# Attention row maxima moved on-chip by one transfer from ScalarE, projections planned half a unit sooner, and another order of the first loads

## The chip, the cores and the metric

The kernel runs on one core of a Trainium2 chip. The time is the device time of one execution in microseconds (us). The core has five engines, each with a queue of its own that it works through in order: TensorE (PE, with its weight loads shown apart as PEld), VectorE (DVE), ScalarE (ACT), GpSimd (POOL) and SyncE (SP). In this kernel SP computes nothing; it issues the DMA transfers. An instruction waits on semaphores for what it needs, and whatever stands behind it in its queue waits with it.

## The reference

Two layers, each of an attention with a compressed memory and a feed-forward part, on x of 2048 rows by 512 columns in float32:

```python
x = x + _A_ref(_layernorm(x, axis=-1), A_wq, A_wk, A_wv, A_wo, A_beta)
x = x + _B_ref(_layernorm(x, axis=-1), B_w_gate, B_w_up, B_w_down)   # (silu(x@wg) * (x@wu)) @ wd, F = 1792
# the same two lines again, with the same weights
```

`_A_ref` projects to q, k and v with 32 heads of 16, and cuts the 2048 rows into 4 segments of 512. Within a segment it is causal softmax attention; across segments each head keeps a 16 by 16 memory that it reads before and updates after a segment. The two results are mixed by a gate, and projected by wo.

## The kernel before, in words

**Precision.** Matmul operands are split into a high and a low part of a reduced format, so each projection takes three passes (`mm3`, L281): 12 matmuls of 128 by 512 for one q or k projection of one group of heads.

**Units.** A layer's attention is 32 units (s, n, h): 4 segments, 4 groups of 8 heads, 2 halves of 4 heads. Here they are counted from 0. Both halves of a group use the same q and k projection. The steps of a unit u are these:

- `qk_proj` (L454) is called for the group two ahead: q in an even unit, k in an odd one. PE makes the 12 matmuls, ACT copies the result out of PSUM (L464), POOL splits it (L465, L467), and SP writes it to a DRAM buffer scrq or scrk, first one part (L479), then two (L480).
- `load3` (L486) reads it back on SP, arranged by heads, into one of three on-chip buffers: cq in two transfers (L504; the trace calls that tile s) and ck in two (L509). As there are three, the load for unit u must wait until the last matmul of unit u-3 has read them.
- `mx_units` (L514) makes the score matmuls for the row maxima (L527); DVE reduces them (L534). `fin` (L541) has PE transpose the 16 by 128 maxima (L544), ACT negate them (L546), and SP write them to DRAM (L547, tile scrm) and read them back as one row of 2048 values into row 127 of cq (L548). That row takes the maximum off the scores in the next matmul.
- `at_units` (L555) makes the transposed score matmuls (L576) into three PSUM banks `plt`, ACT takes their exp (L582), POOL masks the diagonal blocks (L590), and PE multiplies by v (L609).

The feed-forward part (`up`, L856; `down`, L884) is long rows of 512-column matmuls (L866, L893); its first steps and its weight loads (L822) are mixed into the last units of the attention.

**What sets the order.** Nothing is issued as it is written. Every operation is recorded with a cost and a priority, which is a place in time: `at(v)` sets it to v times a unit length T. The tables OFF and PRE (L30, L31) hold these places in units, TA and TF (L29) the lengths for the two parts. `Program.issue` (L144) then plays the program through: on each engine, of the operations that are ready by its own clock, the one with the lowest priority is issued next. The latencies in LAT (L38) and the transfer time in `dma` (L274) say when a result counts as ready. So a changed cost or place reorders all five queues. The start of the first layer loads wv, x, wq, wk and wo (L717 to L728).

Of the kernel before, what the change touches and what calls it, by code (L numbers as in the profile page):

```python
# [8 lines left out]
F32 = mybir.dt.float32  # L9
# [16 lines left out]
LPW = 3  # L26
WOT = ("pmx_0", "pmx_1", "pj", "pj")
EARLY_AT = (23, 25, 26)
TA, TF = 13.82, 15.6  # L29
OFF = {'qe': (0.481, 1.468), 'at': (0.378, 1.18), 'mx': (-0.666, 0.16), 'lf': (-0.709, -0.318), 'mr': (0.865, 0.781), 'mu': (0.556, 0.139), 'wo': (0.263, 1.746), 'qk': (0.158, 0.91), 'v': (-0.3, 0.518), 'lp': (0.034, 1.108)}  # L30
PRE = {'c': -1.851, 'mb': 0.212, 'lv': -2.738, 'lo': -0.87, 'gate': -1.0, 'v': -1.534, 'dv': 0.12, 'qk1': -1.2, 'mx': -1.0}  # L31
EP = {'w': -1.935, 'wn': 0.178, 'ln': -3.0, 'dn': -0.06, 'up': -2.73}
POOL_W = ""
TABLE = 1.28
# [4 lines left out]
    pe=dict(pe=0.01, act=0.2, dve=0.2, sp=0.19),  # L39
    act=dict(act=0.22, dve=0.13, pe=0.27, pool=0.2, sp=0.15),  # L40
    dve=dict(dve=0.13, act=0.13, pe=0.25, pool=0.16, sp=0.12),
    pool=dict(pool=0.1, dve=0.06, pe=0.13, act=0.1, sp=0.05),
    sp=dict(act=0.91, dve=0.91, pe=0.95, pool=0.91, sp=0.91),
)


# [15 lines left out]


class Op:
    __slots__ = ("table", "mode", "eng", "cost", "lat", "fn", "prio", "bufs", "succ", "deps", "ready", "need", "wait", "index")

    def __init__(self, eng, cost, lat, fn, prio, bufs):
        self.eng, self.cost, self.lat, self.fn, self.prio, self.bufs = eng, cost, lat, fn, prio, bufs
        self.mode, self.table = None, None
        self.succ, self.deps, self.ready, self.need, self.wait = [], set(), 0.0, None, 0  # L70


class Program:
# [70 lines left out]
    def issue(self):  # L144
        for b in {id(b): b for o in self.ops for b in o.bufs if b.tag in self.shared}.values():
            first = b.ops[0].index
            need = {d for o in b.ops for d in o.deps if d.index < first}
# [8 lines left out]
        t = dict.fromkeys(engs, 0.65)  # L156
# [8 lines left out]
        done, bus, table, mode = 0, 0.0, "exp", "full"  # L165
        while done < len(self.ops):
            best = None
            for e in engs:
                f, n = fut[e], now[e]
                while True:  # L170
                    while f and f[0][0] <= t[e] + 1e-9:
                        _, i, o = heapq.heappop(f)
                        heapq.heappush(n, (o.prio, i, o))
                    if n:
                        o = n[0][2]
                        b = o.need
                        if b is not None and b.slot is None:
                            if not free[b.tag]:
                                heapq.heappop(n)
                                held[b.tag].append(o)  # L180
                                continue
                            fr = min(free[b.tag])
                            if fr[0] > t[e] + 1e-9:
                                heapq.heappop(n)
                                o.ready = fr[0]
                                heapq.heappush(f, (o.ready, o.index, o))
                                continue
                        start = t[e]
                    elif f:
                        start = f[0][0]  # L190
                        if best is None or start < best[0]:
                            t[e] = start
                            continue
                    else:
                        start = None
                    break
                if start is not None and n and (best is None or start < best[0]):
                    best = (start, e)
            assert best is not None, "no instruction can issue"
            start, e = best  # L200
            n = now[e]
            o = n[0][2]
            heapq.heappop(n)
            b = o.need
            if b is not None and b.slot is None:
                fr = min(free[b.tag])
                free[b.tag].remove(fr)
                b.slot = fr[1]
            for b in o.bufs:
                if b.tile is None:  # L210
                    tag = b.tag if b.slot is None else f"{b.tag}_{b.slot}"
                    b.tile = b.pool.tile(list(b.shape), b.dtype, name=tag, tag=tag)
            o.fn()
            done += 1
            t[e] = start + o.cost
            if o.table and o.table != table:
                table = o.table
                t[e] += TABLE
            if o.mode and o.mode != mode:
                t[e] += DRAIN[mode, o.mode]  # L220
                mode = o.mode
            end = t[e]
            if o.lat:
                bus = max(bus, end + 0.65) + o.lat
                end = bus
            for b in o.bufs:
                b.left -= 1
                if b.left == 0 and b.slot is not None:
                    free[b.tag].append((end + 0.25, b.slot))
                    for w in held[b.tag]:  # L230
                        w.ready = max(w.ready, end + 0.25)
                        heapq.heappush(fut[w.eng], (w.ready, w.index, w))
                    held[b.tag] = []
            for s in o.succ:
                s.ready = max(s.ready, end + LAT[e].get(s.eng, 0.0))
                s.wait -= 1
                if s.wait == 0:
                    heapq.heappush(fut[s.eng], (s.ready, s.index, s))
# [3 lines left out]
def infini_swiglu(ctx: ExitStack, tc: tile.TileContext, x, wq, wk, wv, wo, beta, wg, wu, wd, out,  # L242
                  layers=LAYERS, nseg=NSEG, do_ffn=True):
    nc = tc.nc
    xrows = x.rearrange("b s d -> (b s) d")
    orows = out.rearrange("b s d -> (b s) d")
    pool = ctx.enter_context(tc.tile_pool(name="sb", bufs=1))
# [3 lines left out]
    P = Program({"pj": 2})  # L251
# [20 lines left out]
        op("pool", cost, fn, reads, writes)  # L272

    def dma(fn, reads, writes, kb=256, cost=0.475):  # L274
        op("sp", cost, fn, reads, writes, lat=max(kb / 360, 0.02))

    def mm(ps, view, a, av, b, bv, n, start, stop, passes=1, rk=(None, None)):
        pe(n, passes, lambda: nc.tensor.matmul(view(ps.ap), lhsT=av(a.ap), rhs=bv(b.ap), start=start, stop=stop),  # L278
# [113 lines left out]
    def attention(lay, x_in, x_out, slots, T, hook):  # L392
# [121 lines left out]
        def mx_units(u):  # L514
            f_ = HLF[u]
            cq, ck = f_["cq"], f_["ck"]
            mx = sb("mx", [128, 4, 4], ring=2)

            def head(p, j):
                def f():  # L520
                    for grp in ((0, 1), (2,), (3,)):
                        ps = bank("pmx", ring=2)

                        def fill(ps=ps, grp=grp):
                            for a, qt in enumerate(grp):
                                nk = max(256, 128 * (qt + 1))
                                nc.tensor.matmul(ps.ap[:, a * 256:a * 256 + nk],  # L527
                                                 lhsT=cq.ap[0:127, 2 * j + p, qt * 128:(qt + 1) * 128],
                                                 rhs=ck.ap[0:127, p, 0:nk], start=True, stop=True)
                        pe(384 if grp == (2,) else 512, 1, fill, [(cq, j), (ck, 0), (ck, 1)], [ps], loads=len(grp))  # L530
                        for a, qt in enumerate(grp):
                            w = 128 * (qt + 1)
                            junk = sb("junk", [128, 512], BF16, ring=2)
                            dve(w, lambda a=a, qt=qt, w=w, ps=ps, junk=junk: nc.vector.tensor_tensor_reduce(  # L534
                                out=junk.ap[:, :w], in0=ps.ap[:, a * 256:a * 256 + w], in1=amask.ap[:, 512 - w:],
                                scale=1.0, scalar=-3e38, op0=OP.add, op1=OP.max,
                                accum_out=mx.ap[:, 2 * j + p, qt:qt + 1]),
                                [(ps, a), amask], [junk, (mx, (qt, p, j))])
                return f

            def fin():  # L541
                ps, nm = bank("pj"), sb("nm", [16, 128], F32R, ring=2)
                scr = P.buf(dram, "scrm", [16, 128], F32, ring=2)
                pe(128, 2, lambda: nc.tensor.transpose(ps.ap[:16, 0:128], mx.ap.rearrange("p t h -> p (t h)"),  # L544
                                                       ident.ap), [mx, ident], [ps])
                act(128, lambda: nc.scalar.mul(nm.ap, ps.ap[:16, 0:128], -1.0), [ps], [nm])  # L546
                dma(lambda: nc.sync.dma_start(scr.ap, nm.ap.bitcast(F32)), [nm], [scr], kb=8)  # L547
                dma(lambda: nc.sync.dma_start(  # L548
                    cq.ap[127:128].bitcast(F32).rearrange("o x c -> o (x c)"),
                    scr.ap.rearrange("(o x) c -> o (x c)", o=1)), [scr], [(cq, "m")], kb=8)  # L550
            return [head(p, j) for p in range(2) for j in range(2)] + [fin]

        PARTS = (((0, 0, 0, 512, 0),), ((1, 128, 0, 384, 1), (3, 384, 384, 128, 1), (2, 256, 0, 256, 2)))
# [450 lines left out]
```

## Time and profile before

| what | value |
|---|---|
| median of the three timed runs | 2023.94 us (2022.66 to 2025.35) |
| the profiled execution's own time | 2028.21 us |
| its span, first to last instruction | 2026.3 us |
| mean granted clock of TensorE | 0.994 |
| busy: PE, DVE, ACT, POOL | 1946.7, 1154.0, 770.7, 466.3 us |
| share of the DMA queue's packets in 16 engines' span | 29.7% |

In the lines of a profile, a group shows its line in the kernel, the engine, the operation, and the tiles as out<-in. A row of waits gives who waited for whom, and then the total, the number and the longest, in us. SPq is SP's queue. A row of the timeline begins with start and length in us; a bracket at its end says how long the engine had been idle and what ended that. A row of the table by stretches gives the stretch, its length, then for PE, PEld, DVE, ACT and POOL the busy time and the number of instructions, and at the end the granted clock, the DMA engines' share and GB/s.

### The profile page before, as it was taken

Reading aid. Unit: us, or ns where it says so; the run is one execution under the profiler, and the core shown is the slowest. Engines: PE = TensorE matmul, PEld = TensorE weight load, DVE = VectorE, ACT = ScalarE, POOL = GpSimd, SP = SyncE. Lnnn points to the kernel's source line nnn. Section 1 sums busy time; section 2 is a strip of 40 time slices with the busy share of each in tenths; the row PEclk is TensorE's granted clock in tenths of the full one; section 3 lists DMA queues with packets and bytes.
Section 4 is the critical chain, followed back from the end, with each engine's and each line's share of the span. In section 5 each row is a group of like instructions: output and inputs, shape, how many; then the busy total and the mean of one; then the engine's idle time right before and its main releaser. Section 6 shows DMA issues by size and latency. Waiting matters only on the chain. (4 is left out here: it accounts for less than half of the span.)

```text
span 2026.3 us, 31532 instructions
## 1 busy us (share of the span) xinstructions
PE 1946.7 (96%) x11136; PEld 1481.4 (73%) x11136; DVE 1154.0 (57%) x3446; ACT 770.7 (38%) x1758; POOL 466.3 (23%) x731
## 2 busy tenths in 40 slices
PE   6999999999999999999999899999989999999999
PEld 5667676766678888888866667666757788888887
DVE  5867777767744333333557667776686533333333
ACT  4555565545622212121235545554555212211211
POOL 5333433434410000000233334343343100000000
PEclk9999999999999999999999999999999999999999
DMA  7333434456231100010353344444462301100002
GB/s 221 120 111 119 140 106 142 122 156 190 63 115 32 32 21 18 25 32 21 104 194 111 95 129 124 132 136 122 142 184 64 111 14 32 32 21 11 16 1 83
DMA packets 101677, 184.54 MB, mean 91 GB/s; under 512 B 12880, under 2 KB 28240, under 8 KB 101456
## 3 DMA queue, kind: packets, MB, share of 16 engines
q1 hardware_dynamic: 101520, 182.52, 29.7%
q8 instruction: 89, 1.46, 0.3%
q14 instruction: 68, 0.56, 0.1%
HBM read 114.84 MB, written 67.63 MB: 90 GB/s over the span
## 5 line engine op out<-in xcount | busy, mean ns | idle before, releaser
L534 DVE CUSTOM_DVE_ANT_0 junk<-pmx,amask 128x128 bf16<-128x128 f32 (+3 forms) x1024 | 460.8, 484 | 162.2 <-PE pmx L527 154.2
L866 PE MATMUL plt<-s,s 128*128 128x512 f32 x1872 | 542.9, 395 | 0.0
L278 PE MATMUL pj<-s,s 128*128 128x512 f32 x1416 | 502.4, 410 | 1.4 <-DVE s L898 1.1
L582 ACT ACTIVATE s<-plt 128x512 f32<-128x512 f32 (+2 forms) x768 | 326.3, 464 | 231.3 <-PE plt L576 222.0
L866 PEld LDWEIGHTS plt<-s,s 128*128 128x128 f32 x1872 | 351.6, 188 | 82.0
L527 PE MATMUL pmx<-ck,s 127*128 127x256 f32 (+2 forms) x1024 | 300.5, 347 | 46.3 <-DMA ck<-scrk 35.6
L278 PEld LDWEIGHTS pj<-s,s 128*128 128x128 f32 x1416 | 265.8, 191 | 75.7 <-issue 23.8
L576 PE MATMUL plt<-s,ck 128*128 128x256 f32 (+2 forms) x1024 | 280.1, 339 | 10.4 <-DMA s<-scrm 9.7
L527 PEld LDWEIGHTS pmx<-ck,s 127*128 127x128 f32 x1024 | 183.7, 193 | 126.0 <-issue 50.3
L866 PE MATMUL ppv<-s,s 128*128 128x512 f32 x624 | 245.8, 395 | 0.0
L893 PE MATMUL pj<-s,vt 128*128 128x512 f32 x696 | 211.5, 394 | 0.0
L576 PEld LDWEIGHTS plt<-s,ck 128*128 128x128 f32 x1024 | 180.2, 191 | 38.8 <-DMA s<-scrm 8.3
L893 PE MATMUL pmx<-s,vt 128*128 128x512 f32 x648 | 198.6, 395 | 0.2 <-DVE s L898 0.2
L590 POOL TENSOR_SCALAR_AFFINE_SELECT s<-s 128x512 f32<-128x512 f32 x192 | 124.9, 651 | 267.5 <-ACT s L582 264.4
L876 DVE TENSOR_TENSOR Y<-Y,plt 128x512 f32<-128x512 f32 x52 | 35.8, 688 | 218.2 <-PE plt L866 207.6
L875 ACT ACTIVATE Y<-plt 128x512 f32<-128x512 f32 x52 | 31.1, 598 | 335.2 <-PE plt L866 335.2
L893 PEld LDWEIGHTS pj<-s,vt 128*128 128x128 f32 x696 | 130.7, 188 | 30.6
L893 PEld LDWEIGHTS pmx<-s,vt 128*128 128x128 f32 x648 | 121.6, 188 | 29.0 <-DVE s L898 0.6
L866 PEld LDWEIGHTS ppv<-s,s 128*128 128x128 f32 x624 | 117.4, 188 | 27.3
L609 PE MATMUL ppv<-s,vt 128*32 128x512 f32 (+2 forms) x1536 | 136.7, 458 | 0.0
L876 DVE TENSOR_TENSOR raw<-raw,ppv 128x512 f32<-128x512 f32 x52 | 35.6, 685 | 143.2 <-PE ppv L866 132.6
L898 DVE TENSOR_TENSOR s<-s,pj 128x512 f32<-128x512 f32 x116 | 79.4, 686 | 57.5 <-PE pj L893 56.8
(130 smaller groups left out, 2044.5 us busy)
## 6 DMA issues: line engine op xcount, KB each, us to landing
s<-scrq SPq DMA_DIRECT2D x128, 192.0 KB
ck<-scrk SPq DMA_DIRECT2D x128, 192.0 KB
scrq<-s SPq DMA_DIRECT2D x32, 512.0 KB
scrk<-s SPq DMA_DIRECT2D x32, 512.0 KB
scrq<-s SPq DMA_DIRECT2D x32, 256.0 KB
scrk<-s SPq DMA_DIRECT2D x32, 256.0 KB
xin<-xmid SPq DMA_DIRECT2D x32, 256.0 KB
s<-xmid SPq DMA_DIRECT2D x32, 256.0 KB
```

The costliest lines, as they stand in the source:

```text
L278: pe(n, passes, lambda: nc.tensor.matmul(view(ps.ap), lhsT=av(a.ap), rhs=bv(b.ap), start=start, stop=stop), [(a, rk[0]), (b, rk[1])], [ps])
L527: nc.tensor.matmul(ps.ap[:, a * 256:a * 256 + nk], lhsT=cq.ap[0:127, 2 * j + p, qt * 128:(qt + 1) * 128], rhs=ck.ap[0:127, p, 0:nk], start ...
L534: dve(w, lambda a=a, qt=qt, w=w, ps=ps, junk=junk: nc.vector.tensor_tensor_reduce(out=junk.ap[:, :w], in0=ps.ap[:, a * 256:a * 256 + w], i ...
L576: nc.tensor.matmul(ps.ap[:, c0:c0 + n_], lhsT=ck.ap[:, p, k0:k0 + 128], rhs=cq.ap[:, 2 * j + p, 512 - n_:512], start=True, stop=True)
L582: act(w, lambda Pb=Pb, o0=o0, w=w, i0=i0: nc.scalar.activation(Pb.ap[:, idx, o0:o0 + w], ps.ap[:, i0:i0 + w], AF.Exp, scale=SCALE), [ps], ...
L590: gp(0.593, lambda: nc.gpsimd.affine_select(out=v(), in_=v(), pattern=[[0, 4], [1, 128]], compare_op=OP.is_ge, fill=0.0, base=0, channel_m ...
L609: nc.tensor.matmul(ps.ap[32 * i:32 * i + 32, q0:q0 + w], lhsT=vt.ap[:, kt, VW * hd:VW * hd + 32], rhs=f_[sl].ap[:, idx, c0:c0 + w], start= ...
L866: pe(512, 1, lambda i=i, j=j, kc=kc, x=x, ps=ps, wt=wt: nc.tensor.matmul(ps.ap, lhsT=wt.ap[:, i, kc, cs], rhs=XT[b][j].ap[:, :, kc], start ...
L875: act(512, lambda: nc.scalar.activation(sg.ap, pg.ap, AF.Silu), [pg], [sg], table="silu")
L876: dve(512, lambda: nc.vector.tensor_mul(sg.ap, sg.ap, pu.ap), [sg, pu], [sg])
L893: pe(512, 1, lambda i=i, j=j, fi=fi, x=x, ps=ps, wt=wt, cs=cs: nc.tensor.matmul(ps.ap, lhsT=ht.ap[:, 0:2048].rearrange("p (f a c) -> p f a ...
L898: dve(512, lambda ps=ps, t=t: nc.vector.tensor_add(xb.ap[:, t, :], xb.ap[:, t, :], ps.ap), [ps, (xb, t)], [(xb, t)])
```

## The change

Four things are changed.

- The negated maxima go straight from their tile `nm` to row 127 of cq, in one transfer that ACT starts. The DRAM buffer and the two transfers on SP are gone. A field `post` tells the planner that the result counts as ready 2.2 us later.
- The place of the q and k projections, `qk` in OFF, goes from (0.158, 0.91) to (-0.342, 0.41).
- The place of the wv load, `lv` in PRE, goes from -2.738 to -1.7, behind x, wq and wk, which stand at -2 and -1.95.
- Planner costs: a DMA's latency goes from about 0.9 to 1.2 and its rate from 360 to 250 KB per us; TA and TF go from 13.82 and 15.6 to 15.0 and 16.7.

```diff
-TA, TF = 13.82, 15.6
+TA, TF = 15.0, 16.7
...
-    sp=dict(act=0.91, dve=0.91, pe=0.95, pool=0.91, sp=0.91),
+    sp=dict(act=1.2, dve=1.2, pe=1.2, pool=1.2, sp=1.2),
...
-            end = t[e]
+            end = t[e] + o.post
...
-        op("sp", cost, fn, reads, writes, lat=max(kb / 360, 0.02))
+        op("sp", cost, fn, reads, writes, lat=max(kb / 250, 0.02))
...
             def fin():
                 ps, nm = bank("pj"), sb("nm", [16, 128], F32R, ring=2)
-                scr = P.buf(dram, "scrm", [16, 128], F32, ring=2)
                 pe(128, 2, lambda: nc.tensor.transpose(ps.ap[:16, 0:128], mx.ap.rearrange("p t h -> p (t h)"),
                                                        ident.ap), [mx, ident], [ps])
                 act(128, lambda: nc.scalar.mul(nm.ap, ps.ap[:16, 0:128], -1.0), [ps], [nm])
-                dma(lambda: nc.sync.dma_start(scr.ap, nm.ap.bitcast(F32)), [nm], [scr], kb=8)
-                dma(lambda: nc.sync.dma_start(
-                    cq.ap[127:128].bitcast(F32).rearrange("o x c -> o (x c)"),
-                    scr.ap.rearrange("(o x) c -> o (x c)", o=1)), [scr], [(cq, "m")], kb=8)
+                op("act", 0.1, lambda: nc.scalar.dma_start(
+                    cq.ap[127:128].bitcast(F32).rearrange("o x (t c) -> o (x t) c", t=4),
+                    nm.ap.bitcast(F32)), [nm], [(cq, "m")]).post = 2.2
```

The lines of the changed kernel behind L543 have numbers lower by one to three (L582 becomes L580, L822 becomes L820).

**SP's queue around the loads for unit 26.** Here scrq_3 and scrk_3 hold the projections that units 26 and 27 use, s16 and ck2 are unit 26's cq and ck, s14 is unit 27's cq, and s15 and scrm_1 take the maxima of unit 25. Before:

```order
L822 DMA xn_2_5724<-in_B_w_down_dram 128x512
L479 DMA scrk_3_5739<-s17_5512 128x512
L504 DMA s16_269<-scrq_3_5534 48x2x512 x2
L480 DMA scrk_3_5739<-s17_5512 128x1024
L822 DMA phiq_0_5778<-in_B_w_up_dram 128x2x256
L822 DMA xn_3_5801<-in_B_w_down_dram 128x512
L547 DMA scrm_1_5806<-nm_1_5803 16x128
L509 DMA ck2_288<-scrk_3_5739 48x2x512 x2
L548 DMA s15_235<-scrm_1_5806 1x2048
L504 DMA s14_67<-scrq_3_5534 48x2x512 x2
```

In the change the same loads are s16_238 and ck2_256:

```order
L509 DMA ck1_226<-scrk_2_5224 48x2x512 x2
L479 DMA scrk_3_5514<-s17_5329 128x512
L480 DMA scrk_3_5514<-s17_5329 128x1024
L820 DMA xn_2_5615<-in_B_w_up_dram 128x2x256
L820 DMA phiq_0_5632<-in_B_w_up_dram 128x2x256
L820 DMA xn_3_5653<-in_B_w_up_dram 128x2x256
L504 DMA s16_238<-scrq_3_5333 48x2x512 x2
L509 DMA ck2_256<-scrk_3_5514 48x2x512 x2
L820 DMA xn_2_5745<-in_B_w_down_dram 128x512
L820 DMA xn_3_5759<-in_B_w_down_dram 128x512
```

Both parts of the k write stand ahead of the cq load now, with three weight loads behind them; the ck load follows the cq load at once, and the two transfers of the maxima are gone from the queue.

**ACT's queue where unit 2's maxima are negated.** The L582 or L580 rows are exps of score tiles. Before:

```order
L582 ACTIVATE s13_826<-plt_1_819 128x384
L582 ACTIVATE s13_826<-plt_2_824 128x384
L546 ACTIVATE nm_0_842<-pj_1_834 16x128
L582 ACTIVATE s13_826<-plt_0_846 128x384
L582 ACTIVATE s13_826<-plt_1_856 128x384
L464 COPY raw_870<-pj_0_665 128x512
```

And in the change, where s16_238 is unit 2's cq:

```order
L580 ACTIVATE s13_826<-plt_0_832 128x384
L580 ACTIVATE s13_826<-plt_1_836 128x384
L545 ACTIVATE nm_0_860<-pj_1_853 16x128
L546 DMA s16_238<-nm_0_860 1x16x128
L580 ACTIVATE s13_826<-plt_2_864 128x128
L580 ACTIVATE pc_882<-plt_2_864 128x256
```

The transfer stands in ACT's queue right behind the negation, ahead of the exps. By the order each of these 64 transfers waits for two semaphores, that of ACT's own negation and that of an earlier DMA, the eighth before it in the order of issue.

**SP's queue at the start**, before (s_69 takes wv, s_112 wq, s_122 wk):

```order
L416 DMA s_69<-in_A_wv_dram 128x512 x4
L344 DMA tt_92<-in_A_x_dram 128x512
L344 DMA tt_94<-in_A_x_dram 128x512
L344 DMA phiq_104<-in_A_x_dram 128x512
L344 DMA phiq_107<-in_A_x_dram 128x512
L416 DMA s_112<-in_A_wq_dram 128x512 x4
L416 DMA s_122<-in_A_wk_dram 128x512 x4
```

and in the change (s_129 takes wv):

```order
L344 DMA tt_69<-in_A_x_dram 128x512
L344 DMA tt_75<-in_A_x_dram 128x512
L344 DMA phiq_80<-in_A_x_dram 128x512
L344 DMA phiq_91<-in_A_x_dram 128x512
L416 DMA s_95<-in_A_wq_dram 128x512 x4
L416 DMA s_107<-in_A_wk_dram 128x512 x4
L416 DMA s_129<-in_A_wv_dram 128x512 x4
```

The four loads of wv have moved from the head of the queue to behind those of x, wq and wk.

More of the change, by code (lines that the diff above doesn't have):

```diff
@@ L28 @@
 EARLY_AT = (23, 25, 26)
-TA, TF = 13.82, 15.6
-OFF = {'qe': (0.481, 1.468), 'at': (0.378, 1.18), 'mx': (-0.666, 0.16), 'lf': (-0.709, -0.318), 'mr': (0.865, 0.781), 'mu': (0.556, 0.139), 'wo': (0.263, 1.746), 'qk': (0.158, 0.91), 'v': (-0.3, 0.518), 'lp': (0.034, 1.108)}
-PRE = {'c': -1.851, 'mb': 0.212, 'lv': -2.738, 'lo': -0.87, 'gate': -1.0, 'v': -1.534, 'dv': 0.12, 'qk1': -1.2, 'mx': -1.0}
+TA, TF = 15.0, 16.7
+OFF = {'qe': (0.481, 1.468), 'at': (0.378, 1.18), 'mx': (-0.666, 0.16), 'lf': (-0.709, -0.318), 'mr': (0.865, 0.781), 'mu': (0.556, 0.139), 'wo': (0.263, 1.746), 'qk': (-0.342, 0.41), 'v': (-0.3, 0.518), 'lp': (0.034, 1.108)}
+PRE = {'c': -1.851, 'mb': 0.212, 'lv': -1.7, 'lo': -0.87, 'gate': -1.0, 'v': -1.534, 'dv': 0.12, 'qk1': -1.2, 'mx': -1.0}
 EP = {'w': -1.935, 'wn': 0.178, 'ln': -3.0, 'dn': -0.06, 'up': -2.73}
@@ L64 @@
 class Op:
-    __slots__ = ("table", "mode", "eng", "cost", "lat", "fn", "prio", "bufs", "succ", "deps", "ready", "need", "wait", "index")
+    __slots__ = ("table", "mode", "post", "eng", "cost", "lat", "fn", "prio", "bufs", "succ", "deps", "ready", "need", "wait", "index")
     def __init__(self, eng, cost, lat, fn, prio, bufs):
         self.eng, self.cost, self.lat, self.fn, self.prio, self.bufs = eng, cost, lat, fn, prio, bufs
-        self.mode, self.table = None, None
+        self.mode, self.table, self.post = None, None, 0.0
         self.succ, self.deps, self.ready, self.need, self.wait = [], set(), 0.0, None, 0
```

## The prediction

> **What bounds the kernel now.** The page comes first: span and busy time.
>
> ```profile
> span 2026.3 us, 31532 instructions
> PE 1946.7 (96%) x11136; PEld 1481.4 (73%) x11136; DVE 1154.0 (57%) x3446; ACT 770.7 (38%) x1758; POOL 466.3 (23%) x731
> ```
>
> PE is busy all but 79.6 us, so the change, which leaves every matmul in place, can only give back PE's idle time and time at a low clock. The table by stretches says where PE idles.
>
> ```profile
> 0.00:50.00 50.00, 33.75 (x162) 26.62 (x162) 27.86 (x83) 21.84 (x38) 26.09 (x51) 0.93 0.72 224
> 50.00:550.00 500.00, 474.08 (x3368) 339.36 (x3372) 368.99 (x1364) 277.57 (x696) 198.72 (x305) 0.99 0.43 126
> 550.00:1000.00 450.00, 449.94 (x1971) 363.18 (x1966) 182.99 (x293) 93.52 (x159) 18.18 (x29) 1.00 0.14 46
> ...
> 1050.00:1560.00 510.00, 478.85 (x3406) 342.25 (x3407) 368.89 (x1360) 276.31 (x696) 198.22 (x305) 0.99 0.42 126
> ```
>
> The feed-forward stretch has no idle PE. The start has 16.25 us, the two attention stretches 25.9 and 31.2. PE's waits say for what:
>
> ```profile
> PE pmx L527 <- DMA ck<-scrk: 35.6, 29, 3.9
> PE plt L369 <- ACT xn L358: 11.2, 2, 11.0
> PE plt L576 <- DMA s<-scrm: 9.7, 7, 2.1
> PE pmx L527 <- DVE mx L534: 4.5, 15, 0.6
> PE pmx L527 <- issue: 4.1, 3, 3.4
> ```
>
> So the bound is the landing of DMAs: the projections' way through DRAM (scrk), the maxima's way (scrm), and the first load. All are issued by SP, in order, so I asked what SP itself waits for (total, times, longest).
>
> ```profile
> SPq L547 <- ACT nm L546: 118.0, 48, 7.5
> ...
> SPq L548 <- DMA scrm<-nm: 65.1, 42, 3.5
> SPq L509 <- DMA scrk<-s: 56.6, 23, 6.5
> SPq L504 <- PE plt L576: 47.1, 45, 5.3
> ```
>
> The maxima's two transfers hold the queue 183 us in all. The ck load waits 23 times for the write of k to land, and the c load 45 times for its buffer to be released by the last score matmul of three units earlier. The timeline shows the first kind in unit 26 (counted from 0):
>
> ```profile
> 423.15 0.45 SPq L480 DMA_DIRECT2D scrk<-s  x1
> ...
> 429.89 0.80 SPq L509 DMA_DIRECT2D ck<-scrk  x2
> ...
> 431.30 0.23 SPq L548 DMA_DIRECT2D s<-scrm  x1
> 431.63 0.30 SPq L504 DMA_DIRECT2D s<-scrq  x1
> ...
> 434.11 1.09 PE L527 MATMUL pmx<-ck,s 127*128 127x256 f32 x3 [3.37 <-issue]
> ```
>
> The write of k is issued at 423.15, the load that needs it at 429.89, 6.7 us later; the read of the maxima and a c load for the next unit stand behind it. PE starts at 434.11, 4.2 us after the ck issue, with 3.37 us idle.
>
> **The projections, half a unit sooner.** 32 units lie in about 500 us, so a unit is about 15.6 us and half of it 7.8, more than the longest of the 23 waits (6.5): all 23 go. The order agrees: in unit 26 there are 80 matmuls between the last one of the k projection and the first score matmul, in the new order 158. What is late next is the buffer. Unit 11 shows that case; it is an odd unit, and unit 10 has read the same scrk before it:
>
> ```profile
> 179.75 0.85 SPq L504 DMA_DIRECT2D s<-scrq  x2
> ...
> 181.13 1.41 SPq L509 DMA_DIRECT2D ck<-scrk  x2
> ...
> 187.76 0.47 PE L527 MATMUL pmx<-ck,s 127*128 127x256 f32 x2 [1.39 <-DMA ck<-scrk]
> ```
>
> From the first issue to the matmul it is 8.0 us, with a write of another projection issued in between. This kind stays: 29 less 23 waits are 6, at 35.6/29 = 1.23 us, 7.4 us. The 3.4 us under "issue" is the gap above, of the same kind as the 23, and goes with them. Gain: 35.6 - 7.4 + 3.4 = 31.6 us; bounds 39.7 (all of both rows) and 7 (the buffer rival below). The half unit also moves the projections' writes (L479, L480) past the loads of c and ck on SP, and their copies and splits on ACT and POOL. Idle time covers them, 222 of 500 us on ACT and 301 on POOL; if that cover failed, a late split would eat into the 7.8 us first.
>
> **The clock.** Behind long gaps PE runs at half clock (last but two column):
>
> ```profile
> core 0: 2026.3 us, clock 0.994
> ```
> ```profile
> 495.00:498.50 3.50, 3.50 (x10) 3.02 (x11) 2.02 (x8) 2.29 (x4) 0.00 (x0) 0.52 0.00 0
> ...
> 433.60:437.10 3.50, 2.99 (x9) 2.67 (x10) 1.12 (x6) 0.55 (x2) 0.66 (x2) 0.51 0.08 10
> ...
> 1440.60:1444.00 3.40, 3.40 (x12) 2.92 (x12) 1.70 (x7) 0.55 (x2) 1.22 (x2) 0.50 0.46 128
> 41.00:48.00 7.00, 6.27 (x18) 5.06 (x19) 3.80 (x17) 0.00 (x0) 1.80 (x4) 0.51 0.62 193
> ```
>
> There are five such stretches between 433 and 1444 us, 3.4 us each, so 1.7 us lost in each, 8.5 in all; with 3.4 at the start this is what the mean clock says (0.006 x 2026 = 12.2). I take four as gone: 6.8 us, bounds 0 and 8.5. The Trainium skill (TensorE: Matmul & The Clock Gate, section "What's actually happening") lets the clock fall after an idle window of about 3.4 us; by that only the gap of 3.37 us and one of 3.9 count, this term would be 3.4 and the forecast 1984. The stretch at 495 speaks against it: the gap ahead of it is 1.72 us (row below).
>
> **The maxima, one transfer from ACT.** Two legs now:
>
> ```profile
> 126.16 0.31 SPq L547 DMA_DIRECT2D scrm<-nm  x1
> 127.50 0.23 SPq L548 DMA_DIRECT2D s<-scrm  x1
> ```
> ```profile
> 487.83 0.25 ACT L546 ACTIVATE nm<-pj 16x128 fp32r<-16x128 f32 x1
> ...
> 488.53 0.38 SPq L547 DMA_DIRECT2D scrm<-nm  x1
> ...
> 493.35 0.25 SPq L548 DMA_DIRECT2D s<-scrm  x1
> ...
> 494.98 0.69 PE L576 MATMUL plt<-s,ck 128*128 128x512 f32 x1 [1.72 <-DMA s<-scrm]
> ```
>
> The first leg takes 1.34 us undisturbed and 4.8 where other loads stand between; the second 1.6. One leg in place of two brings the row 1.3 to 4.8 us sooner; the longest of the 7 waits is 2.1. Of 9.7 us I take 8.7, bounds 0 and 9.7. No transfer between two on-chip tiles is in the trace; its price is taken as one leg, 1.3 to 4.8 us. 128 issues leave SP. ACT gets 64, at SP's price:
>
> ```profile
> L547 SPq DMA_DIRECT2D scrm<-nm x64: 312/328/1077, 53.1 to 1530.9; - x64
> ```
> ```profile
> L576 PE MATMUL plt<-s,ck 128*128 128x256 f32 (+2 forms) x1024 | 280.1, 339 | 10.4 <-DMA s<-scrm 9.7
> ```
>
> 64 x 0.33 = 21 us on ACT, beside its idle 222 of each 500 us. Queued behind each are the exps of the next score tiles; three PSUM banks of them lie between ACT and PE. I take 2 us on PE, bounds 0 and 21 (all of it on the path).
>
> **The start.** wv loads first now:
>
> ```profile
> 3.45 1.28 ACT L417 CAST s<-s 128x512 fp32r<-128x512 f32 x2 [1.39 <-DMA s<-in_A_wv_dram]
> ...
> 6.15 0.62 ACT L417 CAST s<-s 128x512 fp32r<-128x512 f32 x1 [0.43 <-DMA s<-in_A_wv_dram]
> ...
> 7.41 1.28 DVE L349 BATCH_NORM_STATS2 bst<-tt 128x6 f32<-128x512 f32 x2
> ...
> 11.04 2.34 PE L369 MATMUL plt<-ident,xn 128*128 128x128 f32 x8 [11.04 <-ACT xn L358]
> ```
>
> With x first, its first tile lands where wv's does now, 3.96 us sooner, and the first transpose follows at 7.1. wv's four tiles land 0.9 us apart ((6.15 - 3.45)/3), so behind twelve others its last is there near 17 us (3.45 + 15 x 0.9); the 24 matmuls of q and k go ahead of the v projection and cover that, and without that cover PE would idle at most the 4 us won. The first unit's loads still go through DRAM, and part of the time won on the way there may only lengthen PE's wait for them. I take 3 us, bounds 0 and 4.
>
> **The new order elsewhere.** The planner's costs for DMA rise, so every queue is reordered a little. With 45 us less, DVE is busy 369 of about 477 us per stretch in place of 500. I let PE's waits for DVE (4.5 us) double: 4.5 us, bounds 0 and 12. The new T values scale all times of a stage alike and cost nothing.
>
> **Sum.** 31.6 + 6.8 + 8.7 + 3 - 2 - 4.5 = 43.6 us. The profiled execution took 2028.2 us, 1.9 more than its span, and 4.3 more than the median of the three timed runs, 2023.9. From that median: 1980.
>
> **Rivals.** *The buffer ends last everywhere.* The c load's 45 waits for its release already outnumber the 23 for the write. If what follows the release (8.0 us in unit 11) always ends just behind the write, the sooner projection gives a tenth of the 35.6 us and the 3.4, 7 in all, and the clock 1.7. Then 7 + 1.7 + 8.7 + 3 - 6.5 = 13.9: 2010. Against it: the 8.0 us contain a foreign write, which the new order puts ahead. Chance 0.14.
>
> *The small transfer queues anyway.* The engines that move the 192 KB loads move the maxima too; 16 rows behind four loads in flight land late, whoever starts them. The 8.7 us stay lost: 1989. Chance 0.07; 1.34 us in the row above speaks against it. The Trainium skill has this as a rule (DMA: Bandwidth & Descriptors, section "Issuing engines are not separate DMA queues"): starting transfers on more engines only saves time on the sequencer.
>
> *ACT stands at its transfers: slower.* The transfer waits for the maxima and, by the order, for an earlier DMA's semaphore; the exps behind it wait too. SP stood 1.55 us (65.1/42) at such a wait. If ACT stood 1.55 + 0.33 at all 64, and three score tiles of 0.27 us (280.1/1024) covered 0.8, PE would lose 1.1 x 64 = 70 us: 2024 - 45.6 + 70 = 2048 (45.6 being the sum without ACT's 2). It decides from 0.7 us a unit. Against it: the earlier DMA is the eighth before, about a unit back. Chance 0.08.
>
> *The waits only change their names.* Landing is set by traffic (share 0.43), and freed queues issue into it: no change, 2024. Chance 0.05.
>
> **Numbers.** My forecast has 0.66, its own range 1962 (all upper bounds, 62 us) to 1994 (the clock at 3.4 us, ACT's cost 8, the new order's 9). The range 1960 to 2012 takes in the buffer rival and leaves out the last two. Faster by over 0.2% (4 us, about what a measurement of this kernel can tell from none): 0.66 + 0.14 + 0.07 = 0.87; same 0.05; slower 0.08.
>
> **What would show it.** Right: ck<-scrk under 10 us among PE's waits, no wait for the maxima over 2 us, one or no half-clock stretch between 433 and 1444 us, the first transpose near 7 us, a span near 1983. Wrong: ck waits still near 30 us with SP's c loads waiting for plt (the buffer); PE waiting on plt or s from ACT, with ACT idle ahead of its transfer (the slower rival); waits for DVE over 10 us (the new order).

## The result and the profile after

| | before | after |
|---|---|---|
| median of the runs, us | 2024.64 (4 runs) | 1979.19 (4 runs, 1975.99 to 1981.12) |
| ratio, 95% interval | | 0.977 (0.9748 to 0.9793) |
| profiled execution, us | 2028.21 | 1979.63 |
| its span, us | 2026.3 | 1977.9 |
| mean granted clock | 0.994 | 0.997 |

The change is 2.3% faster, 45 us. The forecast was 1980, so the number came out; the sections below show that the reason given for the largest part of it did not. Of the ten executions of one kernel below, the one with the load order alone, one took 2673 us at a granted clock of 0.656; it is counted in that kernel's median and not in its ratio. First the page of the changed kernel, its span and busy time.

```profile
span 1977.9 us, 31484 instructions
...
PE 1933.5 (98%) x11136; PEld 1472.8 (74%) x11136; DVE 1141.8 (58%) x3446; ACT 768.4 (39%) x1758; POOL 471.4 (24%) x731
```

PE's idle time fell from 79.6 to 1977.9 - 1933.5 = 44.4 us, and its busy time by 13.2 us, of which the clock makes about half (0.006 x 2026.3 = 12.2 us lost before, 0.003 x 1977.9 = 5.9 now). The table by stretches puts the saving where the prediction looked for it.

```profile
0.00:50.00 50.00, 37.47 (x175) 28.71 (x175) 31.09 (x88) 22.80 (x41) 28.10 (x53) 0.93 0.75 239
50.00:550.00 500.00, 489.17 (x3473) 351.00 (x3473) 373.55 (x1379) 278.01 (x698) 201.69 (x308) 1.00 0.43 130
550.00:1000.00 450.00, 448.37 (x1960) 364.77 (x1959) 185.32 (x305) 95.59 (x165) 25.66 (x43) 1.00 0.15 47
1050.00:1560.00 510.00, 498.75 (x3484) 360.06 (x3483) 370.83 (x1324) 273.45 (x681) 199.62 (x306) 1.00 0.43 129
```

The attention stretches idle 10.8 and 11.3 us, in place of 25.9 and 31.2; the start does 3.7 us more work in its 50 us. PE's waits:

```profile
PE pmx L527 <- DMA ck<-scrk: 7.4, 11, 3.3
PE pmx L527 <- DVE mx L534: 7.3, 18, 1.0
PE plt L369 <- ACT xn L358: 6.6, 1, 6.6
...
PE plt L574 <- DMA s<-nm: 1.4, 3, 0.6
```

The waits for ck went from 35.6 to 7.4 us, those for the maxima from 9.7 to 1.4. Among SP's own waits (total, times, longest), the ck load hardly waits for the write of k any more (56.6 us before), and the c load waits longer for its buffer:

```profile
SPq L504 <- PE pmx L527: 103.3, 50, 9.4
...
SPq L509 <- DMA scrk<-s: 9.7, 6, 2.9
```

The groups of PE's instructions give the idle time ahead of the two kinds of score matmuls (behind the second bar). First before, then after.

```profile
L527 PE MATMUL pmx<-ck,s 127*128 127x256 f32 (+2 forms) x1024 | 300.5, 347 | 46.3 <-DMA ck<-scrk 35.6 <-DVE mx L534 4.5 <-issue 4.1
```
```profile
L527 PE MATMUL pmx<-ck,s 127*128 127x256 f32 (+2 forms) x1024 | 299.3, 346 | 17.6 <-DMA ck<-scrk 7.4 <-DVE mx L534 7.3 <-issue 1.1
L574 PE MATMUL plt<-s,ck 128*128 128x256 f32 (+2 forms) x1024 | 269.6, 334 | 1.8 <-DMA s<-nm 1.4
```

At L527 28.7 us went, ahead of the transposed scores 8.6 (10.4 less 1.8), ahead of the first transpose 4.6. The prediction's terms for these places were 31.6, 8.7 and 3. Everything it named as a sign of being right is there. None of these signs tells which of the four edits did it, since all four were made at once. That is what the experiments ask.

### The profile page after: what moved, and what is told of

Read it like the earlier page. It is cut to its first block, busy times and chain, and to the rows that moved or that the text cites. A ratio compares the mean times of both kernels' runs of the same rounds, so it can differ in the third digit from the quotient of the medians.

```text
span 1977.9 us, 31484 instructions
## 1 busy us (share of the span) xinstructions
PE 1933.5 (98%) x11136; PEld 1472.8 (74%) x11136; DVE 1141.8 (58%) x3446; ACT 768.4 (39%) x1758; POOL 471.4 (24%) x731
## 5 line engine op out<-in xcount | busy, mean ns | idle before, releaser
L864 PE MATMUL plt<-s,s 128*128 128x512 f32 x1872 | 535.9, 393 | 2.2 <-ACT s L373 2.2
L278 PE MATMUL pj<-s,s 128*128 128x512 f32 x1416 | 483.9, 409 | 0.1
L580 ACT ACTIVATE s<-plt 128x512 f32<-128x512 f32 (+2 forms) x768 | 330.6, 469 | 208.8 <-PE plt L574 189.2
L527 PE MATMUL pmx<-ck,s 127*128 127x256 f32 (+2 forms) x1024 | 299.3, 346 | 17.6 <-DMA ck<-scrk 7.4
L574 PE MATMUL plt<-s,ck 128*128 128x256 f32 (+2 forms) x1024 | 269.6, 334 | 1.8 <-DMA s<-nm 1.4
L527 PEld LDWEIGHTS pmx<-ck,s 127*128 127x128 f32 x1024 | 179.7, 190 | 91.5 <-DVE mx L534 23.4
L574 PEld LDWEIGHTS plt<-s,ck 128*128 128x128 f32 x1024 | 175.1, 189 | 33.7 <-ACT s L580 12.0
L891 PE MATMUL pj<-s,vt 128*128 128x512 f32 x696 | 180.3, 394 | 0.6 <-DVE s L896 0.6
L891 PE MATMUL pmx<-s,vt 128*128 128x512 f32 x648 | 164.6, 393 | 0.0
L351 POOL TENSOR_SCALAR bmv<-bmv 128x1 f32<-128x1 f32 x64 | 16.7, 262 | 500.7 <-DVE bmv L350 499.6
```

The source lines that it names most:

```text
L351: gp(0.18, lambda: nc.gpsimd.tensor_scalar_add(mv.ap[:, 1:2], mv.ap[:, 1:2], EPS), [mv], [mv])
L527: nc.tensor.matmul(ps.ap[:, a * 256:a * 256 + nk], lhsT=cq.ap[0:127, 2 * j + p, qt * 128:(qt + 1) * 128], rhs=ck.ap[0:127, p, 0:nk], start ...
L574: nc.tensor.matmul(ps.ap[:, c0:c0 + n_], lhsT=ck.ap[:, p, k0:k0 + 128], rhs=cq.ap[:, 2 * j + p, 512 - n_:512], start=True, stop=True)
L580: act(w, lambda Pb=Pb, o0=o0, w=w, i0=i0: nc.scalar.activation(Pb.ap[:, idx, o0:o0 + w], ps.ap[:, i0:i0 + w], AF.Exp, scale=SCALE), [ps], ...
L864: pe(512, 1, lambda i=i, j=j, kc=kc, x=x, ps=ps, wt=wt: nc.tensor.matmul(ps.ap, lhsT=wt.ap[:, i, kc, cs], rhs=XT[b][j].ap[:, :, kc], start ...
L891: pe(512, 1, lambda i=i, j=j, fi=fi, x=x, ps=ps, wt=wt, cs=cs: nc.tensor.matmul(ps.ap, lhsT=ht.ap[:, 0:2048].rearrange("p (f a c) -> p f a ...
```

## The experiments

The four parts are called the projections (`qk` in OFF), the load order (`lv` in PRE), the planner's numbers (TA, TF, the DMA latency and rate) and the transfer (the maxima on-chip, with `post`). The ratios are to the kernel before in runs on the same chip (2027 to 2028 us).

### The projections alone, and all but the projections

Added alone to the kernel before:

```diff
-'qk': (0.158, 0.91)
+'qk': (-0.342, 0.41)
```

> The kernel before with one edit: the place of the q and k projections half a unit sooner. Projection theory (PE's waits for ck come from the late write of k): 31.6 us of ck waits and 6.8 us of half clock go, 2024 - 38 = about 1986; ck<-scrk falls from 35.6 to about 8 us among PE's waits, scrm<-nm waits stay near 10. Queue theory (the two transfers of the maxima on SP hold up the loads behind them): 2012 to 2020, ck<-scrk stays over 20 us. Cost theory (the planner's higher DMA costs made an order that covers the transfers): 2010 or more.

Measured: 2028.38 us, ratio 1.0004 (0.9989 to 1.0019). PE's waits and SP's wait for the write of k:

```profile
PE pmx L527 <- DMA ck<-scrk: 18.3, 16, 3.6
PE pmx L527 <- DVE mx L534: 17.6, 36, 1.4
```
```profile
SPq L509 <- DMA scrk<-s: 3.7, 3, 1.7
```

The mechanism of the prediction works as described: SP's 23 waits for the write are 3, 56.6 us are 3.7. The time does not move. PE's waits for ck are halved (17.3 us less), and the waits for VectorE's maxima grow by most of that (13.1 us); the idle time ahead of L527 falls by 3.8 us only:

```profile
L527 PE MATMUL pmx<-ck,s 127*128 127x256 f32 (+2 forms) x1024 | 305.9, 351 | 42.5 <-DMA ck<-scrk 18.3 <-DVE mx L534 17.6 <-DVE r L624 1.4
```

The other way round, the changed kernel with the projections where they were:

```diff
-'qk': (-0.342, 0.41)
+'qk': (0.158, 0.91)
```

> The changed kernel without the half unit: projections back at their old place, all else changed. Projection theory: the ck waits come back, 1979 + 38 = about 2015, ck<-scrk near 30 us. Queue theory: 1985 to 1992, since the maxima stay off SP. Cost theory: 1980 to 1992, since the costs are still the new ones.

Measured: 1980.80 us, ratio 0.9772 (0.974 to 0.9805), as fast as the whole change. PE's waits, and SP's:

```profile
PE pmx L527 <- DMA ck<-scrk: 8.8, 7, 3.1
```
```profile
SPq L509 <- DMA scrk<-s: 58.7, 23, 5.7
```

This is the plainest answer of the study. SP waits for the write of k as often and as long as in the kernel before, 23 times and 58.7 us, and PE waits only 8.8 us for ck all the same. A wait of the DMA queue is no wait of PE, as long as PE's own order does not come to the score matmuls before the load has landed.

### The planner's numbers alone, and all but these

Added alone (and, in the second kernel, taken out of the changed one):

```diff
-TA, TF = 13.82, 15.6
+TA, TF = 15.0, 16.7
-sp=dict(act=0.91, dve=0.91, pe=0.95, pool=0.91, sp=0.91)
+sp=dict(act=1.2, dve=1.2, pe=1.2, pool=1.2, sp=1.2)
-lat=max(kb / 360, 0.02)
+lat=max(kb / 250, 0.02)
```

> The kernel before with the planner's numbers alone: DMA latency 1.2, 250 KB per us, TA and TF 15.0 and 16.7. Cost theory (the order that the higher costs make covers the transfers, whatever the place of the projections): 1965 to 1980, ck<-scrk under 12 us. Combination theory (the costs work only together with the sooner projections or the sooner first loads): 2000 or more.

Measured alone: 2000.19 us, ratio 0.9866 (0.9843 to 0.9888). No transfer and no place of the program is another, only the order (ACT has 1762 instructions in place of 1758, four more loads of its function tables). The idle time ahead of L527 falls nearly as far as in the whole change (17.6 us), and the waits for the maxima go as well, 0.7 us in place of 9.7, though these still take the two transfers through DRAM:

```profile
L527 PE MATMUL pmx<-ck,s 127*128 127x256 f32 (+2 forms) x1024 | 301.1, 348 | 19.8 <-DVE mx L534 11.9 <-DMA ck<-scrk 4.7 <-issue 2.1
L576 PE MATMUL plt<-s,ck 128*128 128x256 f32 (+2 forms) x1024 | 276.4, 336 | 3.1 <-ACT pc L582 1.6 <-DMA s<-scrm 0.7 <-ACT s L582 0.4
```

> The changed kernel with the planner's old numbers: projections, loads and maxima changed. Cost theory: 2010 to 2022, ck<-scrk near 30 us, about what the transfer of the maxima alone gave (2018.7). Combination theory: 1985 to 2000.

Measured without them: 2000.32 us, ratio 0.9866 (0.9835 to 0.9896).

```profile
L527 PE MATMUL pmx<-ck,s 127*128 127x256 f32 (+2 forms) x1024 | 299.7, 347 | 27.6 <-DMA ck<-scrk 13.2 <-DVE mx L534 9.2 <-issue 4.1
```

So the numbers bring 27 us alone, and about 20 us of the 45 are lost when they are missing. The prediction had put 4.5 us of loss here. They are not the only way to the 28.7 us ahead of L527: without them the other three edits together still take off 18.7 (46.3 less 27.6). The latency, the rate and the two unit lengths were not tried one by one.

### One belief of the planner

The sharpest form of this: the kernel before, in which the two transfers of each ck load count as landed 1.5 us later. Nothing else is changed.

```diff
-                end = bus
+                end = bus + o.post
...
-                    [g["scrk"]], [(ck, j)], kb=196)
+                    [g["scrk"]], [(ck, j)], kb=196).post = 1.5
```

> The kernel before with only one number of the planner different: the two transfers of each ck load count as landed 1.5 us later. No place of the projections, no transfer, no other cost is changed. Theory of the belief: PE stands because the planner puts the score matmuls where it believes ck to be there, and an honest time makes it put other ready work there. Then PE's waits for ck fall from 35.6 us to under 12, and the time by 15 us or more: ratio under 0.9925. Theory of the prediction: only a sooner write of k helps; the waits stay near 30 us and the ratio is 1.000. Theory of mere scatter (any new order moves the time by some 8 us either way): ratio between 0.996 and 1.004 with other waits in place of those for ck.

Measured: 1999.43 us, ratio 0.9861 (0.9844 to 0.9879): 28 us from one number. PE's waits, then SP's for the write:

```profile
PE plt L576 <- DMA s<-scrm: 10.7, 6, 3.1
PE pmx L527 <- DVE mx L534: 5.0, 18, 0.5
PE pmx L527 <- DMA ck<-scrk: 3.5, 5, 1.1
```
```profile
SPq L509 <- DMA scrk<-s: 46.0, 24, 4.5
```

The waits for ck are nearly gone (35.6 to 3.5 us), those for the maxima are as before (9.7, now 10.7), and SP still waits 24 times for the write. The timeline shows how, in the unit that the prediction had taken as its case, unit 26 (its ck load is the row at 419.51):

```profile
419.38 0.50 PE L278 MATMUL pj<-s,s 128*128 128x512 f32 x1
419.51 0.80 SPq L509 DMA_DIRECT2D ck<-scrk  x2
419.72 0.40 PE L576 MATMUL plt<-s,ck 128*128 128x256 f32 x2
419.95 0.39 PE L278 MATMUL pj<-s,s 128*128 128x512 f32 x1
...
421.11 0.39 PE L659 MATMUL pj<-mb,phiq 128*128 128x136 f32 x2
...
423.59 0.47 PE L576 MATMUL plt<-s,ck 128*128 128x512 f32 x1 [1.39 <-DMA s<-scrm]
423.90 0.58 PE L527 MATMUL pmx<-ck,s 127*128 127x256 f32 x3
```

In the kernel before PE had 3 matmuls left when the ck load was issued (429.89) and then stood 3.37 us; here it has 16, projections and scores of other units, and the gap of 1.39 us that is left ends with the maxima. The first score matmul follows the issue by 4.4 us here and by 4.2 there. The load did not get quicker; PE has work while it is under way. Counted over the 64 units, the first score matmul starts within 4 us of the end of the ck issue in 23 units before, 13 here, 4 in the changed kernel. The page of the changed kernel gives what a load takes from issue to landing (columns: tile, transfers, KB, median us):

```profile
ck<-scrk SPq DMA_DIRECT2D x128, 192.0 KB, 4.2
```

The planner before counted 0.65 + 196/360 + 0.95 = 2.1 us behind the issue, and after the change 0.65 + 196/250 + 1.2 = 2.6. The profile of the kernel before has no landing times for this load; the kernel further below with its order and the on-chip transfer has 4.0 us. So the load took about as long in both orders. The change raises this belief by 0.5 us, the experiment by 1.5: it shows that such a belief is enough, not that the 0.5 us do it in the change.

### More of the same

If 1.2 helps, more might help more: the latency at 1.7, in the fastest kernel of this study (below).

```diff
-sp=dict(act=1.2, dve=1.2, pe=1.2, pool=1.2, sp=1.2)
+sp=dict(act=1.7, dve=1.7, pe=1.7, pool=1.7, sp=1.7)
```

> The fastest kernel so far (sooner projections, load order and planner's costs, but the maxima still in two transfers on SP; 1968 us, ratio 0.971) with the planner's latency of a DMA at 1.7 in place of 1.2. A ck load takes 4.2 us from issue to landing in the changed kernel (median); the planner counts 0.65 + 196/250 + 1.2 = 2.6 us at 1.2 and 3.1 at 1.7. If the belief is still too short, the 7 us of waits for ck shrink further and the time goes to about 1962 us, ratio 0.968. If waits and late work already balance, it stays between 1965 and 1980 us, ratio 0.970 to 0.977, with the waits for DVE grown in their place.

Measured: 1990.60 us, ratio 0.9819 (0.9802 to 0.9836), against 0.9709 at 1.2. Both theories missed the time: 1.7 is slower by over 1%.

```profile
PE pmx L527 <- DVE mx L534: 11.7, 30, 0.8
...
PE pmx L527 <- DMA ck<-scrk: 3.1, 2, 2.8
```

The waits for ck do shrink, from 7.1 to 3.1 us, and those for VectorE grow from 8.6 to 11.7. That makes no 22 us. PE is idle for 8.6 us more in all (45.5 against 36.9), and busy for 13 us more (1942.5 against 1929.2), of which the lower clock (0.995 against 0.997) makes about 4. What lengthens the rest is open. In this version a higher number is worse; two values show no more than that.

### The transfer alone, and all but the transfer

The edit of `fin` and of `post` as shown in the change, alone:

```diff
-                dma(lambda: nc.sync.dma_start(scr.ap, nm.ap.bitcast(F32)), [nm], [scr], kb=8)
...
+                op("act", 0.1, lambda: nc.scalar.dma_start(
...
+                    nm.ap.bitcast(F32)), [nm], [(cq, "m")]).post = 2.2
```

> The kernel before with one edit: maxima in one transfer started by ACT. Projection theory: 8.7 us of maxima waits and perhaps one or two half-clock stretches go, ACT costs 2: 2014 to 2018; ck<-scrk stays near 35 us. Queue theory: with SP's queue free the ck waits fall under 15 us, 1985 to 1995.

Measured: 2018.67 us, ratio 0.996 (0.9944 to 0.9976), 8 us faster. And the change without it (the same lines, removed and added the other way round):

> The changed kernel with the maxima's two transfers through DRAM back on SP, all else changed. Projection theory: 7 to 10 us come back, 1986 to 1990, ck<-scrk under 12 us and scrm waits near 8 us. Queue theory: the loads are held up again, 2005 or more, ck<-scrk over 20 us.

Measured: 1968.07 us, ratio 0.9709 (0.9683 to 0.9735). It beats both kernels: without the transfer the change is 11 us faster than with it.

```profile
PE pmx L527 <- DVE mx L534: 8.6, 26, 0.7
...
PE pmx L527 <- DMA ck<-scrk: 7.1, 8, 2.6
```
```profile
L576 PE MATMUL plt<-s,ck 128*128 128x256 f32 (+2 forms) x1024 | 267.4, 332 | 1.2 <-ACT s L582 0.8
```

PE's waits have no row for the maxima at all, though they go the long way through DRAM. So the same edit gains 8 us alone and costs 11 beside the other three; each time the planner also makes another order. Two kernels with a fixed order tell the transfer from the order that comes with it.

### The transfer with the order held

The planner is told of the two old transfers; in the place of the first, ACT starts the on-chip one, in the place of the second nothing is issued. The queues of PE, DVE and POOL are those of the kernel before.

```diff
-                dma(lambda: nc.sync.dma_start(scr.ap, nm.ap.bitcast(F32)), [nm], [scr], kb=8)
-                dma(lambda: nc.sync.dma_start(
-                    cq.ap[127:128].bitcast(F32).rearrange("o x c -> o (x c)"),
-                    scr.ap.rearrange("(o x) c -> o (x c)", o=1)), [scr], [(cq, "m")], kb=8)
+                dma(lambda: nc.scalar.dma_start(
+                    cq.ap[127:128].bitcast(F32).rearrange("o x (t c) -> o (x t) c", t=4),
+                    nm.ap.bitcast(F32)), [nm], [scr], kb=8)
+                dma(lambda: None, [scr], [(cq, "m")], kb=8)
```

> The kernel before with only the maxima's transfer exchanged: ACT starts one on-chip transfer at the place in the program where SP had recorded the first leg, and SP's two transfers are gone. The queues of PE, DVE and POOL stand row for row as before, so no new order can help or harm. If the transfer itself brings what the prediction took (8.7 us of waits gone, 2 us lost behind ACT's issues), the time falls by 6.7 us: ratio 0.9967, about 2018 us, with no wait of PE for s<-nm above 2 us. If the 8 us that the same edit brought when it was made alone came from the new order, the ratio is 1.000 (2025 us). If ACT's 64 issues of 0.51 us lie on the path, it is slower, up to 1.016.

Measured: 2014.55 us, ratio 0.9936 (0.992 to 0.9952): 13 us (10 to 16), from the transfer alone.

```profile
L527 PE MATMUL pmx<-ck,s 127*128 127x256 f32 (+2 forms) x1024 | 298.8, 345 | 45.2 <-DMA ck<-scrk 18.2 <-issue 11.8 <-DVE mx L534 6.7
L576 PE MATMUL plt<-s,ck 128*128 128x256 f32 (+2 forms) x1024 | 277.8, 336 | 0.7 <-ACT pc L582 0.4 <-ACT s L582 0.2
```

The idle time ahead of L576 falls from 10.4 to 0.7 us, which is the 9.7 us of waits in the prediction's row, and 4 more come with the clock (0.994 to 0.996). The idle time ahead of L527 stays (46.3, now 45.2): with 128 transfers fewer in SP's queue the scores still stand where they stood.

The second: the changed kernel, with SP in ACT's place as the starter.

```diff
-                op("act", 0.1, lambda: nc.scalar.dma_start(
+                op("act", 0.1, lambda: nc.sync.dma_start(
```

> The changed kernel with one word different: SP starts the maxima's on-chip transfer in place of ACT, at the same place in the program. PE, DVE and POOL have the same queues row for row. The kernel that kept the two old transfers beside the three other edits was 11 us faster than the changed kernel. If that is what ACT loses by starting the transfers (64 x 0.51 = 33 us, a third of it on the path), this kernel runs at 1968 us, ratio 0.972. If it came from the other order that the planner finds, ACT's issues cost nothing and the time is that of the changed kernel, 1979 us, ratio 0.977, or a little more, if SP's queue delays the maxima.

Measured: 1976.45 us, ratio 0.9747 (0.973 to 0.9764). The changed kernel had 0.977 (0.9748 to 0.9793); the intervals overlap. The kernel with SP as starter is 3 us faster by the medians and 5 by the ratios, and by the intervals anything from nothing to 10 us. It is still 8 us slower than the kernel with the two old transfers, so most of the 11 us are not what ACT pays for starting transfers. With the transfer itself a gain in the order of before, what remains for them is the other order. That last step is argued; the two old transfers in the changed kernel's order were not run.

### The load order alone, and all but the load order

```diff
-'lv': -2.738
+'lv': -1.7
```

> The kernel before with the wv load behind x, wq and wk, nothing else. First theory (the start gains 3 us): 2021 to 2024 against 2027 of the kernel before on that chip. Rival (the first unit still waits for its way through DRAM): no change within 2 us, the first score matmul still near 41 us.

Measured alone: 2023.61 us, ratio 0.9975 (0.9957 to 0.9994), 5 us faster (1 to 9). Where its first score matmul stood is not shown.

> The changed kernel with the wv load first again. First theory: 3 us slower, 1982. Rival: within 2 us of 1979.

Measured in the changed kernel with the old load order: 1984.68 us, ratio 0.9789 (0.9761 to 0.9817), about 4 us slower than with the new one (0.977); the intervals overlap, so this size is not clear of noise. As far as they go, alone and left out agree.

## Why the prediction was right, and where it was wrong

**The step that failed** is the largest term: "32 units lie in about 500 us, so a unit is about 15.6 us and half of it 7.8, more than the longest of the 23 waits (6.5): all 23 go." SP's waits did go. The step that does not follow is the next, that PE's waits go with them, 31.6 us in the sum. The sooner projections alone are worth nothing (1.0004), taken out of the change they cost nothing (0.9772 against 0.977), and PE's waits for ck are as short with SP's 58.7 us of waits as without them. The prediction's rival that the waits only change their names was given 0.05 for the whole kernel; for this part it is what happened, with VectorE's 17.6 us as the new name. What can bring nearly all of it is the term that it had dismissed, "every queue is reordered a little", priced at a loss of 4.5 us: the planner's numbers alone take 26.5 us of idle time off L527 (46.3 to 19.8) and 27 us off the kernel, and one belief on the ck load, later by 1.5 us, gives 28. Of the 18.7 us that the other three edits take off without these numbers, the projections alone make 3.8 and the transfer alone 5.4 (46.3 to 40.9); what makes the rest was not run. So that 31.6 was forecast for this place and 28.7 came is luck. The wait named a DMA, and as far as the traces show the DMA was as long as ever (4.0 and 4.2 us); what was wrong in the order of before was the place of the matmuls in PE's queue. The prediction read the row "ck<-scrk" as a late load, and could as well have read it as an early matmul.

**The buffer.** That the c load's wait for its release is next was right. The row that the prediction shows is one of three for PE: SP waited 47.1 us at plt, 42.9 at pmx and 39.0 at pj before, 129 in all, and 58.4, 103.3 and 67.0 now, 229 in all. PE's waits for ck were 7.4 us with it, so it did as little harm there as the wait for the write.

**The transfer.** 8.7 us of waits were forecast as won. In the order of before the transfer wins 9.7. In the whole change 8.6 us of idle time went at that place, but the transfer need not have done it: the planner's numbers alone leave 0.7 us of waits for the maxima, and with the two old transfers beside the other three edits 1.2 us of idle time is left there and none of it for the maxima. ACT's 2 us can't be told from none, as the kernel with SP as starter is 3 to 5 us faster with overlapping intervals. ACT did not stand: its longest wait for a semaphore at the transfer was 38 ns. The price of an issue was wrong, as the rows of the changed kernel and of the one with SP as starter show (min, median and longest in ns):

```profile
L546 ACTq EVENT_SEMAPHORE  x65: 17/17/38, 52.2 to 1481.3; - x65
L546 ACTq DMA_DIRECT2D s<-nm x64: 510/511/585, 52.5 to 1481.6; - x64
```
```profile
L546 SPq DMA_DIRECT2D s<-nm x64: 508/515/970, 52.3 to 1478.2; - x64
```

0.51 us, not the 0.33 of the old write, on either engine: 33 us of ACT's time rather than 21. That the changed kernel would be 11 us faster with the old transfers, in the order that the new numbers make of them, was in no rival.

**The small transfer queues anyway**: hardly. It lands 1.9 us after its issue in the median, 5.0 at the most:

```profile
DMA to landing us min/median/max: 1.8/1.9/5.0
```

**The start.** The first transpose was forecast for 7.1 us and came earlier still:

```profile
6.63 3.25 PE L369 MATMUL plt<-ident,xn 128*128 128x128 f32 x12 [6.63 <-ACT xn L358]
...
41.59 1.09 PE L527 MATMUL pmx<-ck,s 127*128 127x256 f32 x3 [3.33 <-DMA ck<-scrk]
```

3 us were forecast; 5 were measured alone and 4, not clear of noise, in the change, and the 3.7 us of work more in the first 50 us agree. As the prediction feared, the first unit did not start sooner for it: 41.59, with 3.33 us of wait for ck, against 41.23 with 3.40 before.

```profile
41.23 1.08 PE L527 MATMUL pmx<-ck,s 127*128 127x256 f32 x3 [3.40 <-DMA ck<-scrk]
```

What is won there is other PE work that was done by then: 175 matmuls in the first 50 us, against 162.

**The clock.** None of the five half-clock stretches between 433 and 1444 us is left, and a new one has come at 1047; by the mean clocks 6.3 us are won, against the 6.8 of the forecast.

**The sum.** Alone, the four parts give 0, 27, 5 and 8 us (13 with the order held), 40 to 45 in all, against 45 measured. That it adds up so well is partly luck: three of them together without the planner's numbers give 27 us where their single gains make 13 to 18, and leaving the transfer out gains 11. A new order moves this kernel by 10 us and more (11 slower with the transfer, 22 slower with the latency at 1.7), whatever the edit is for; why these orders differ so was not settled.

## What to carry to other kernels

Where a planner sets the order, a wait for a load has two readings, a late load or a consumer placed too early; make the planner believe a later landing for that one load before moving anything else. A term that fits the row where the time goes away says nothing of which edit sent it away: try each part alone and the whole without it. And once several edits reorder the queues, try the whole without each, since one that gains alone can cost in company, as the transfer did here; of the kernels run here the version without it is the fastest (1968 us).

## What was not expected of the hardware

The half-clock stretches lie on a grid. By the clock's records those of the kernel before begin at 433.67, 495.11, 508.77, 1147.06 and 1440.61 us; the distances are whole multiples of 3.413 us (495.11 - 433.67 = 61.44 = 18 x 3.413), and each lasts one step. In these traces PE has idle time in the window of the grid ahead of such a stretch, but that window need not be idle throughout. The windows ahead of the five, and one more (busy PE time is the number behind the length):

```profile
430.25:433.66 3.41, 0.49 (x4) 0.16 (x2) 0.00 (x0) 1.26 (x6) 1.27 (x1) 1.00 0.80 175
491.69:495.10 3.41, 1.66 (x12) 1.16 (x12) 2.35 (x11) 0.59 (x1) 0.00 (x0) 1.00 0.49 148
505.35:508.76 3.41, 1.35 (x10) 1.02 (x7) 2.47 (x11) 0.13 (x1) 1.43 (x3) 1.00 0.71 149
1143.65:1147.06 3.41, 0.24 (x2) 0.28 (x3) 0.00 (x0) 0.67 (x3) 1.22 (x2) 1.00 0.48 118
1208.50:1211.90 3.40, 1.69 (x10) 1.18 (x11) 1.59 (x4) 0.60 (x1) 0.63 (x1) 1.00 0.65 192
1437.20:1440.60 3.40, 0.77 (x6) 0.48 (x5) 0.00 (x0) 1.31 (x6) 1.27 (x1) 1.00 0.35 105
```

In the five PE is busy for 7 to 49% of the window. In the one at 1208.5 it is busy for 50%, and no half clock follows. The Trainium skill (TensorE: Matmul & The Clock Gate, section "What's actually happening") has the window, 3413 ns and free-running, and the trace agrees; it names an idle window as the condition, and the trace does not: 1.66 busy microseconds of 3.41 were too few. The changed kernel leaves no sharp bound: its one stretch, at 1047.3, follows a window that was busy for 2.08 of 3.40 us (61%), and behind the window of the same grid that ends at 98.4, busy for 1.56 us (46%), the clock stays full:

```profile
95.00:98.40 3.40, 1.56 (x12) 1.33 (x11) 3.40 (x10) 2.60 (x7) 1.24 (x2) 1.00 0.55 225
1043.90:1047.30 3.40, 2.08 (x10) 1.33 (x10) 3.40 (x11) 2.91 (x8) 2.29 (x3) 1.00 0.49 196
```

So a gap far shorter than 3.4 us can cost 1.7 us more, half of a stretch of 3.4: it was 1.72 us ahead of 495.11, and ahead of 1047.3 one of 1.03 and one of 0.29. Another of 1.71 us, in the window from 1208.5, cost nothing. What decides between them is open.
